# Half-height row tiles in the feed-forward products of a float32 transformer block on one Trainium2 core

## The chip, the cores and the metric

One of the eight cores of a Trainium2 chip runs the whole program. The metric is the device time of one launch in microseconds (us), as the median of the runs shown. Inputs and outputs are float32 in device memory. TensorE (PE in the profile) multiplies, VectorE (DVE), ScalarE (ACT) and GpSimd (POOL) do the element-wise work, and SyncE (SP) issues the transfers.

## The reference

A pre-layer-norm block over 2048 rows of 448 columns: multi-query attention with 16 heads of 28, then a SwiGLU feed-forward of width 1792.

```python
h  = x + A(_layernorm(x), wq, wk, wv, wo)        # attention, not touched by the change
h2 = h + B(_layernorm(h), w1, w3, w2)

def _B_ref(x, w1, w3, w2):                       # x 2048x448, w1 and w3 448x1792, w2 1792x448
    gate = jnp.einsum("bsd,df->bsf", x, w1)
    up   = jnp.einsum("bsd,df->bsf", x, w3)
    return jnp.einsum("bsf,fd->bsd", _silu(gate) * up, w2)
```

## The kernel before

Every float32 operand of a product is split into a high part, rounded to the matmul's float32r type, and a low part, the rest. A product of two such operands is the sum of three: high times high, low times high and high times low.

The rows of x are cut into 4 tiles of 512 (`t`), the feed-forward width into 14 chunks of 128 (`k`). The feed-forward runs over 4 x 14 = 56 blocks `(t, k)`, in order. In each block:

- `split_w` splits the columns of w1 and w3 for the chunk two blocks ahead (cast on VectorE, rest on GpSimd), and `split_w2` the rows of w2 for the next chunk. Split weights of w1 and w3 lie in a ring of seven `qs` buffers, those of w2 in the two places of `w2s`.
- `ffn1` makes the gate and the up products, each in a PSUM bank of its own (named `pa`), with `mm_D`: 448 contraction rows are three chunks of 128 and one of 64. The three chunks give 9 matmuls (three pairs of parts). For the last chunk the low part of x stands in partitions 0 to 63 and the high part in 64 to 127 of `xh[:, 3]`, and the weights stand there twice, so 2 matmuls do it. That is 11 matmuls of 512 columns for each bank, 22 in the block.
- Then ScalarE takes SiLU of the gate bank, VectorE multiplies it with the up bank, ScalarE rounds the result (`h[:, 0]`) and VectorE subtracts it to get the low part (`h[:, 1]`). These four steps write the tiles `pt`.
- `ffn2` takes the hidden part of the previous block (`prev`) times w2, into four banks `Y` (named `pb`) of 128 rows by 448 columns: 4 x 3 = 12 matmuls. `Y` collects over the 14 chunks of a row tile. After its last chunk `y_out` adds each bank to `X` on VectorE, and SyncE stores it.

Pieces of other work are hung on blocks in the table `after`: the output projection of the last attention rows (`wo_rows`, 11 full matmuls each), statistics and normalisation of the next row tile (`ln_stats`, `ln_norm`), and its transposes (`ln_tr`, 4 matmuls for each 128 columns, one column group in each of the blocks 5 to 8).

Seven PSUM banks are handed out by `bank`, which takes the free one whose last use is expected to end first. The eighth held the attention's output.

In the attention, the scores and row maxima (`Head.mm` and `Unit.mm`, lines 367 and 283) already use TensorE in four tiles of 32 rows, with up to four matmuls next to each other. All matmuls of the feed-forward use the full 128 rows.

Of the kernel before, what the change touches and what calls it, by code (L numbers as in the profile page):

```python
# [8 lines left out]
F32 = mybir.dt.float32  # L9
F32R = mybir.dt.float32r  # L10
AF = mybir.ActivationFunctionType
ALU = mybir.AluOpType
# [4 lines left out]
P = 128  # L17
S = 2048
D = 448
# [3 lines left out]
T = 512  # L23
NT = S // T
NQ = T // P
NG = H // 4
NC = S // P
NF = F // P
# [7 lines left out]
def block_kernel(  # L36
# [13 lines left out]
    ve, se, ge, pe, sy = nc.vector, nc.scalar, nc.gpsimd, nc.tensor, nc.sync  # L50
# [4 lines left out]
    def f(ap):  # L55
        return ap.bitcast(F32)
# [24 lines left out]
    W13, W2 = {}, dict(enumerate(W2_0))  # L81
    homes, n_qs = list(range(4)), [0]

    def qs_tile():
        k, n_qs[0] = homes[n_qs[0] % len(homes)], n_qs[0] + 1
        return keep.tile([P, 2, T], F32R, name="qs", tag=f"q{k}")
# [51 lines left out]

    clock, ready = Clock(), {}
    free, used = list(range(7)), {}  # L140
    order = [0.0] * 7

    def bank(name="pb"):
        k = min(free, key=lambda k: order[k])
        free.remove(k)
        ps = ps_w.tile([P, T], F32, name=name, tag=f"bank{k}")
        used[id(ps)] = ps, k
        ready.pop(id(ps), None)
        return ps

    def done(ps, at=None):
        k = used.pop(id(ps))[1]
        order[k] = ready.get(id(ps), clock.end) + 0.7 if at is None else at
        free.append(k)
# [29 lines left out]
    LN = {}  # L184
# [28 lines left out]
    XT = {}  # L213

    def xt_tiles():
        return [xt_pool.tile([P, m, T], F32R, name=name) for m, name in ((4, "xh"), (3, "xl"))]
# [11 lines left out]
    def ln_tr(t, c, spare=False):  # L228
        ps = last = TB[c] if TB else bank()
        if c == 0:  # L230
            XT[t] = xt_tiles()
        xh, xl = XT[t]
        r, c0 = (slice(0, P), c * P) if c < 3 else (slice(64, P), D - P)
        xns = LN[t][3]
        for n in range(NQ):
            if TB:
                break
            pe.transpose(ps[:, n * P : (n + 1) * P], xns[n][:, c0 : c0 + P], ident)  # L238
            clock.mm("full", 0, ps, 0.109, n == 0)
        se.activation(xh[r, c], ps[r], AF.Copy)  # L240
        eng = ve
        if spare:
            x32 = wk_pool.tile([P, T], F32, name="rb")
            se.activation(x32[r], ps[r], AF.Copy)
            eng, ps = ge, x32
        if c < 3:
            eng.tensor_tensor(xl[:, c], ps, f(xh[:, c]), op=ALU.subtract)
        else:
            eng.tensor_tensor(xh[:64, 3], ps[r], f(xh[r, 3]), op=ALU.subtract)
        if TB and c == 3:  # L250
            TB.clear()
        done(last)


    QS, MX, MR, PT, PO, WH, WS = {}, {}, {}, {}, {}, {}, {}
# [17 lines left out]
    class Unit:  # L273
# [22 lines left out]
        def plain(self):  # L296
            self.ps = self.mm()
            self.red()
# [102 lines left out]
    def o_norm(g):  # L401

        sm, sd = SM.pop(g), dr_pool.tile([4, T], F32, name="sd")
        ve.reciprocal(sm, sm)
        sy.dma_start(sd.rearrange("j (b e) -> (j b) e", b=32), sm)
        rb = RB[g] = wk_pool.tile([P, T], F32, name="rb")
        for j in range(4):
            sy.dma_start(rb[32 * j : 32 * j + 32], sd[j : j + 1].to_broadcast([32, T]))
# [37 lines left out]
    w2s_home = []  # L446

    def split_w2(k):
        if k == 0 and not w2s_home:
            w2s = qs_tile()  # L450
        else:
            if not w2s_home:
                w2s_home.append(keep.tile([P, 2, 2, T], F32R, name="w2s", tag="ks1"))
            w2s = w2s_home[0][:, k % 2]
        ve.tensor_copy(w2s[:, 0, :D], W2[k])
        ge.tensor_tensor(w2s[:, 1, :D], W2[k], f(w2s[:, 0, :D]), op=ALU.subtract)
        return w2s

    PAIRS = (0, 1)
# [10 lines left out]
    with tc.tile_pool(name="start", bufs=1) as sp:  # L470
# [106 lines left out]
        first = plain(0, 0, 0) + plain(0, 0, 1) + diffs(0, 0, 2) + plain(0, 1, 1) + sums(0, 0, 2) + plain(0, 1, 0) + diffs(0, 0, 3) + sums(0, 0, 3) + diffs(1, 0, 0) + sums(1, 0, 0) + plain(0, 2, 0) + plain(0, 2, 2) + plain(0, 2, 1) + plain(0, 3, 2) + plain(0, 3, 0) + diffs(0, 2, 3) + sums(0, 2, 3) + plain(0, 3, 1) + [(max_done, 0)] + diffs(1, 2, 0) + [(max_rows, 0), (max_out, 0)] + sums(1, 2, 0)  # L577
# [12 lines left out]
        po = ps_o.tile([P, T], F32, name="po")  # L590
# [189 lines left out]
    def pt_ring():  # L780
        k, n_ring[0] = n_ring[0] % 4, n_ring[0] + 1
        return pt_new(k)
# [20 lines left out]
    for t in range(NT - 1):  # L803
# [6 lines left out]
        for n in range(NQ):  # L810
# [8 lines left out]
            late = NC * NG * (t + 2) + 14 if t < 2 else LAST - 12  # L819
# [16 lines left out]
    for s in range(AHEAD, LAST):  # L836
        i, c = divmod(s, NC)
        n, kt = divmod(c, NQ)
# [7 lines left out]
    units = [0] + [64 - 4 * (AHEAD - NC)] + [64] * (NI - 2)  # L846
# [119 lines left out]

    HID, Y = {}, {}
    o_norm(NG - 1)

    def ffn1(t, k, W):  # L970
        ps = [bank("pa"), bank("pa")]
        for m in range(2):
            mm_D(ps[m], ps[m], [w[:, :, 1 - m] for w in W], XT[t], slice(0, P), slice(0, T))
        sg = f(pt_ring()[:, 0])
        se.activation(sg, ps[0], AF.Silu)  # L975
        done(ps[0])
        ve.tensor_tensor(sg, ps[1], sg, op=ALU.mult)  # L977
        done(ps[1])
        h = pt_ring()
        se.activation(h[:, 0], sg, AF.Copy)  # L980
        ve.tensor_tensor(h[:, 1], sg, f(h[:, 0]), op=ALU.subtract)  # L981
        HID[t, k] = h[:, 0], h[:, 1]

    def ffn2(t, k, n):
        if n == 0 and k == 0:
            Y[t] = [bank() for _ in range(NQ)]
        hid, w2s = HID[t, k], WS[t, k]
        for m, (a, b) in enumerate(((0, 0), (1, 0), (0, 1))):
            pe.matmul(Y[t][n][:, :D], hid[a][:, n * P : (n + 1) * P], w2s[:, b, :D],  # L989
                      start=(k == 0 and m == 0), stop=(k == NF - 1 and m == 2))  # L990

    def y_out(t, n):
        ve.tensor_tensor(X[t][:, n], Y[t][n][:, :D], X[t][:, n], op=ALU.add)  # L993
        done(Y[t][n])
        if t == NT - 1:
            sy.dma_start(ov[t][:, n], X[t][:, n])
        elif n == NQ - 1:
            sy.dma_start(ov[t], X[t])

    tl = NT - 1  # L1000
    after = {}

    def on(t, k, fn, *args):
        after.setdefault((t, k), []).append((fn, args))

    on(0, 0.5, o_mul, tl, NG - 1)
    on(0, 2, o_split, tl, NG - 1, lambda o, i: se.activation(o, i, AF.Copy), ve)
    for k in range(2):
        on(0, 2.5, load_w13, 2 * tl + k)
    for n in range(NQ):  # L1010
        on(0, 3 + n / 2, wo_rows, tl, n)
        on(0, 5 + n, ln_stats, tl, n)
    on(0, 4.5, put_late)
    for k in range(8, NF):
# [3 lines left out]
    for t in range(1, NT):  # L1018
        for n in range(NQ):
            on(t - 1, 1 + n, ln_norm, t, n)  # L1020
        for c in range(4):
            on(t - 1, 5 + c, lambda t, c: ln_tr(t, c), t, c)

    prev = None
    for t in range(NT):
        for k in range(NF):
            end = t == tl and k >= NF - 2
            t2, k2 = divmod(NF * t + k + 2, NF)
            if t2 < NT:
                WH[t2, k2] = split_w(k2)  # L1030
            ffn1(t, k, WH.pop((t, k)))
            for fn, args in after.get((t, k), []):
                fn(*args)
            if prev is not None and not end:
                for n in range(NQ):
                    ffn2(*prev, n)
                if prev[1] == NF - 1:
                    for n in range(NQ):
                        y_out(prev[0], n)
            t2, k2 = divmod(NF * t + k + 1, NF)  # L1040
            if t2 < NT and not end:
                WS[t2, k2] = split_w2(k2)
            for fn, args in after.get((t, k + 0.5), []):
                fn(*args)
            prev = (t, k)
    for n in range(NQ):
        ffn2(tl, NF - 3, n)
# [34 lines left out]
```

## Time and profile before

| | |
|---|---|
| median of 3 runs | 1179.75 us (1178.96 to 1179.86) |
| the profiled execution | 1180.76 us, of which the span of the profile is 1179.0 us |
| TensorE busy | 1168.7 us, 99% of the span |
| TensorE weight loads | 748.5 us, 63%, beside the matmuls |
| VectorE, ScalarE, GpSimd busy | 784.5, 745.1 and 325.3 us |
| attention | up to 742 us |
| feed-forward | from 742 us to the end |

Line numbers are those of the kernel before. In the profile a matmul's own time overlaps with the next one's, so what a matmul costs is read from how far apart starts lie, or from the chain of work that ended last, which gives each piece the time until the next one took over. PEld is the load of the stationary operand. A name such as `pb<-w2s,pt` says which tile is written and which are read.

### The profile page before, as it was taken

How to read it: one execution, taken by the hardware profiler on the slowest of the kernel's cores; microseconds unless marked ns; L12 is line 12 of the kernel's file. 1: busy time of each engine (PE TensorE's matmuls, PEld its weight loads, DVE VectorE, ACT ScalarE, POOL GpSimd, SP SyncE). 2: the span in 40 equal slices, each digit the busy share in tenths (PEclk: the TensorE clock that was granted, in tenths of full speed). 3: DMA queues.
4: the chain of work that ended last, by engine and by line, in shares of the span. 5: the costliest groups of instructions: out<-in, count | busy, mean ns of one | idle time of the engine just before them, and what ended most of it. 6: DMA issues, size and time to landing. Idle time of an engine off the chain costs nothing.

```text
span 1179.0 us, 22184 instructions
## 1 busy us (share of the span) xinstructions
PE 1168.7 (99%) x8618; PEld 748.5 (63%) x8618; DVE 784.5 (67%) x1479; ACT 745.1 (63%) x1435; POOL 325.3 (28%) x240
## 2 busy tenths in 40 slices
PE   8999999999999999999999999999999999999998
PEld 6664444445444445444455443788888888888887
DVE  7878999897899988989987961454343333333332
ACT  5649999996999997999997999312112211211111
POOL 5312001111110111110113013335555445455552
PEclk9999999999999999999999999999999999999999
DMA  4010100011000001000011000242000000000000
GB/s 165 10 37 1 42 10 11 19 22 39 19 19 5 16 24 38 19 19 13 9 39 35 6 18 19 70 113 69 1 32 1 1 4 28 1 1 32 1 1 31
DMA packets 35049, 30.58 MB, mean 26 GB/s; under 512 B 11904, under 2 KB 29568, under 8 KB 34944
## 3 DMA queue, kind: packets, MB, share of 16 engines
q1 hardware_dynamic: 34944, 29.17, 8.6%
q8 instruction: 67, 1.10, 0.4%
q14 instruction: 38, 0.31, 0.1%
HBM read 20.37 MB, written 3.80 MB: 20 GB/s over the span
## 4 chain that ended last, share of the span: by engine, by line
PE 93%; ACT 2%; DVE 2%; DMA 1%; issue 1%; SPq 0%; POOLq 0%; POOL 0%; ACTq 0%; DVEq 0%
PE pa L163 26%; PE po L383 21%; PE pb L367 20%; PE pb L989 11%; PE pa L283 10%; PE pb L163 4%; PE pb L238 1%; ACT OT L390 1%; DVE mx L293 1%; ACT ab L304 1%; ACT pt L374 0%; DMA sd<-sm 0%; DMA X<-in_A_x_dram 0%; DVE pt L981 0%; DVE X L993 0%
## 5 line engine op out<-in xcount | busy, mean ns | idle before, releaser
L293 DVE TENSOR_REDUCE mx<-pa 128x1 f32<-128x512 f32 x689 | 440.4, 685 | 21.9 <-PE pb L367 12.9
L367 PE MATMUL pb<-qs,KS 32*128 32x512 f32 x3072 | 385.3, 425 | 0.0
L374 ACT ACTIVATE pt<-pb 128x512 f32<-128x512 f32 x684 | 365.9, 620 | 12.5 <-PE pb L367 9.4
L367 PEld LDWEIGHTS pb<-qs,KS 32*128 32x128 f32 x3072 | 233.9, 182 | 133.4 <-ACT pt L374 68.1
L283 PE MATMUL pa<-KS,qs 32*128 32x512 f32 x886 | 312.1, 459 | 1.4
L163 PE MATMUL pa<-xh,qs 128*128 128x512 f32 x896 | 231.2, 390 | 0.0
L283 PEld LDWEIGHTS pa<-KS,qs 32*128 32x128 f32 x886 | 138.9, 182 | 82.8 <-DVE mx L293 46.4
L163 PEld LDWEIGHTS pa<-xh,qs 128*128 128x128 f32 x896 | 168.1, 188 | 33.8 <-issue 0.8
L383 PE MATMUL po<-pt,VA 128*32 128x512 f32 x1368 | 182.2, 604 | 0.4 <-ACT pt L374 0.4
L977 DVE TENSOR_TENSOR pt<-pa,pt 128x512 f32<-128x512 f32 x56 | 38.7, 691 | 206.9 <-PE pa L163 202.3
L975 ACT ACTIVATE pt<-pa 128x512 f32<-128x512 f32 x56 | 33.5, 599 | 193.0 <-PE pa L163 193.0
L989 PE MATMUL pb<-w2s,pt 128*128 128x448 f32 x660 | 144.4, 367 | 1.0 <-DVE pt L981 0.8
L414 POOL TENSOR_TENSOR OT<-OT,rb 128x512 f32<-128x512 f32 x15 | 19.2, 1282 | 456.3 <-DMA rb<-sd 251.6
L980 ACT ACTIVATE pt<-pt 128x512 fp32r<-128x512 f32 x56 | 35.4, 632 | 153.6 <-DVE pt L977 149.4
L989 PEld LDWEIGHTS pb<-w2s,pt 128*128 128x128 f32 x660 | 122.9, 188 | 13.4 <-DVE pt L981 1.2
L311 DVE CUSTOM_DVE_ANT_0 ab<-pa,ab 128x512 f32<-128x512 f32 x138 | 93.7, 687 | 39.8 <-PE pa L283 32.6
L374 ACT ACTIVATE xl<-pb 128x512 f32<-128x512 f32 x170 | 99.5, 609 | 7.6 <-PE pb L367 5.5
L374 ACT ACTIVATE xh<-pb 128x512 f32<-128x512 f32 x170 | 104.2, 631 | 0.0
L163 PE MATMUL pa<-xl,qs 128*128 128x512 f32 x336 | 94.5, 389 | 0.0
L383 PE MATMUL po<-xh,VA 128*32 128x512 f32 x340 | 89.4, 605 | 0.0
L383 PE MATMUL po<-xl,VA 128*32 128x512 f32 x340 | 89.4, 605 | 0.0
L304 ACT ACTIVATE ab<-pa 128x512 f32<-128x512 f32 x138 | 82.3, 608 | 6.6 <-PE pa L283 4.8
(109 smaller groups left out, 1088.8 us busy)
## 6 DMA issues: line engine op xcount, KB each, us to landing
rb<-sd SPq DMA_DIRECT2D x64, 64.0 KB
QR<-OT SPq DMA_DIRECT2D x60, 56.0 KB
QR<-in_B_w_dram SPq DMA_DIRECT2D x16, 192.0 KB
X<-in_A_x_dram SPq DMA_DIRECT2D x3, 896.0 KB
out_dram<-X SPq DMA_DIRECT2D x3, 896.0 KB
w<-in_B_w_dram SPq DMA_DIRECT2D x8, 192.0 KB
w_wo<-in_B_w_dram SPq DMA_DIRECT2D x6, 224.0 KB
qs<-mr SPq DMA_DIRECT2D x64, 2.0 KB
```

What stands on the lines that cost most here:

```text
L163: pe.matmul(ps, lhs[b][:, cb, lsl], rhs[a][:, ca, rsl], start=(k == 0), stop=(k == len(terms) - 1),)
L283: pe.matmul(ps, QS[i][r, 0, n * P : (n + 1) * P], KS[0][r, kt * T : (kt + 1) * T] if keys is None else keys[r], start=True, stop=True)
L293: ve.tensor_reduce(self.to(), ps, axis=AX.X, op=ALU.max)
L304: se.activation(self.ab, ps, AF.Relu)
L311: ve.tensor_tensor_reduce(self.ab, ps, self.ab, 1.0, -3.0e38, ALU.add, ALU.max, self.to())
L367: pe.matmul(self.ps, KS[k % 2][r, c * P : (c + 1) * P], QS[i][r, k // 2], start=(k == 0), stop=(k == 2))
L374: se.activation(f(PT[i, c, p][:, jj]), self.ps, AF.Exp, bias=0.0, scale=SCALE)
L383: pe.matmul(PO[i][32 * j : 32 * j + 32], VA[:, c], f(PT[i, c, j // 2][:, j % 2]), start=(c == 0), stop=(c == NC - 1))
L975: se.activation(sg, ps[0], AF.Silu)
L977: ve.tensor_tensor(sg, ps[1], sg, op=ALU.mult)
L980: se.activation(h[:, 0], sg, AF.Copy)
L989: pe.matmul(Y[t][n][:, :D], hid[a][:, n * P : (n + 1) * P], w2s[:, b, :D], start=(k == 0 and m == 0), stop=(k == NF - 1 and m == 2))
```

## The change

Fifty of the 56 blocks, from block 4 of the first row tile to block 11 of the last, are done in tiles of 64 contraction rows. TensorE is used as two halves: half 0 works on partitions 0 to 63, half 1 on 64 to 127, and `two` issues their matmuls in turn, one for each half, into different banks.

The order in such a block is: phase one of the first product (`ffn1_half`, gate in half 0 and up in half 1, 11 matmuls each), phase one of the second product of the previous block (`ffn2_half`, 6 each), phase two of the first (up in half 0 and gate in half 1, 10 each), the element-wise chain (`hidden`), phase two of the second (6 each). Counted in pairs, that is 21 pairs of 512 columns and 12 pairs of 448 columns.

Each bank is thus written by one half in one phase and by the other half in the other. Between the phases `settle` has ScalarE read one element of the bank into a scratch tile, and the next phase's first matmul into that bank waits for that read.

For the 64 last contraction rows half 0 also needs the high part of x, which stands in partitions 64 to 127: `put_xd` copies it down once for each row tile (ScalarE).

The transposes of the next row tile are done in halves too (`tr_half`, two column groups in each of blocks 5 and 7, half of them in each phase). `y_out` leaves two of the four banks of the first three row tiles to ScalarE (copy to `xn`) and GpSimd (addition), and in that block `y_out` stands between the multiplication and the rounding of the hidden part. The eighth bank is handed out as well. Each split part of w2 starts 16 floats further on in its buffer. Two pieces of `wo_rows` move from the steps 4 and 4.5 of the first row tile to 3 and 3.5.

```diff
+    order[7] = clock.end + 4
...
+    def two(pairs):
+        for units in zip(*pairs):
+            for h, (ps, lhs, rhs, first, last) in enumerate(units):
+                pe.matmul(ps[:, : rhs.shape[-1]], lhs, rhs, start=bool(first), stop=bool(last), skip_group_check=True)
...
+    def settle(ps):
+        se.activation(pexp[:1, 8:9], ps[:1, :1], AF.Copy)
...
+    def products(t, W, m, h):
+        r = HALF[h]
+        u = [(W[b][r, c, 1 - m], XT[t][a][r, c]) for a, b in PAIRS3 for c in range(3)]
+        return u + [(W[0][r, 3, 1 - m], XT[t][0][r, 3])]
+
+    def ffn1_half(t, k, W, ps, late):
+        us = [products(t, W, late, 0), products(t, W, 1 - late, 1)]
+        if not late:
+            extra = W[1][HALF[0], 3, 1], XD[0][HALF[0]]
+            us[0].insert(0 if k == NF - 1 else len(us[0]), extra)
+            us[1].append((W[1][HALF[1], 3, 0], XT[t][0][HALF[1], 3]))
...
+    def ffn2_half(t, k, late):
...
+        for h in range(2):
+            for n0 in (2, 0) if late else (0, 2):
+                n, r = n0 + (h ^ late), HALF[h]
+                for m, (a, b) in enumerate(PAIRS3):
+                    us[h].append((Y[t][n], hid[a][r, n * P : (n + 1) * P], w2s[r, b],
...
+        two(us)
+        settle(Y[t][0 if late else 3])
...
     def y_out(t, n):
-        ve.tensor_tensor(X[t][:, n], Y[t][n][:, :D], X[t][:, n], op=ALU.add)
+        y, eng = Y[t][n][:, :D], ve
+        if t < NT - 1 and n > 1:
+            y, eng = ln_pool.tile([P, 512], F32, name="xn", bufs=4)[:, :D], ge
+            se.activation(y, Y[t][n][:, :D], AF.Copy)
+        eng.tensor_tensor(X[t][:, n], y, X[t][:, n], op=ALU.add)
...
+                ps = [bank("pa"), bank("pa")]
+                ffn1_half(t, k, W, ps, 0)
+                call(between, t, k)
+                ffn2_half(*prev, 0)
+                ffn1_half(t, k, W, ps, 1)
+
+                def rest():
+                    ffn2_half(*prev, 1)
+                    call(behind, t, k)
+                    if prev[1] == NF - 1:
+                        for n in range(NQ):
+                            y_out(prev[0], n)
+
+                hidden(t, k, ps, rest if prev[1] == NF - 1 else None)
+                call(after, t, k)
+                if prev[1] != NF - 1:
+                    rest()
```

The order of TensorE in one block before: `pa` are the two banks of the first product, `xh` and `xl` the high and low part of x, `qs` the split w1 and w3, `pt` the hidden part.

```order
L163 MATMUL pa<-xh,qs 128x512 x3
L163 MATMUL pa<-xl,qs 128x512 x3
L163 MATMUL pa<-xh,qs 128x512 x8
L163 MATMUL pa<-xl,qs 128x512 x3
L163 MATMUL pa<-xh,qs 128x512 x5
L989 MATMUL pb<-w2s,pt 128x448 x12
```

One block now, from the fifth matmul of `ffn2_half`'s first phase to the block's end, with what a row waits for on other engines. Each row holds matmuls of both halves in turn, and all banks have the same names as before:

```order
L992 MATMUL pb<-w2s,pt 128x448 [waits Pool_49]
L992 MATMUL pb<-w2s,pt 128x448 x7
L992 MATMUL pa<-xh,qs 128x512 [waits Activation_49]
L992 MATMUL pa<-xh,qs 128x512 x5
L992 MATMUL pa<-xl,qs 128x512 x6
L992 MATMUL pa<-xh,qs 128x512 x8
L992 MATMUL pb<-w2s,pt 128x448 [waits Activation_49]
L992 MATMUL pb<-w2s,pt 128x448 x11
```

The 22 matmuls of the first product became two runs of 22 and 20 half-height ones, of which the second stands here, between two runs of 12 of the second product; the first matmul of a run now waits for ScalarE, whose `settle` reads one of its banks after the run before.

VectorE around the last addition of the first row tile, before: `X_77` is that row tile, `pt<-pa,pt` the multiplication and `pt<-pt` the subtraction of the hidden part.

```order
L977 TENSOR_TENSOR pt<-pa,pt 128x512
L981 TENSOR_TENSOR pt<-pt 128x512
L993 TENSOR_TENSOR X_77<-pb,X_77 128x448 x4
L455 CAST w2s<-w2r_100 128x448
L442 CAST qs<-QR_89 128x1024
```

And now, at the same place:

```order
L1002 TENSOR_TENSOR pt<-pa,pt 128x512
L1079 TENSOR_TENSOR X_77<-pb,X_77 128x448 x2
L1008 TENSOR_TENSOR pt<-pt 128x512
L462 CAST w2s<-w2r_100 128x448
L449 CAST qs<-QR_89 128x1024
```

Two of the four additions left VectorE, and the other two moved ahead of the subtraction that ends the hidden part.

More of the change, by code (lines that the diff above doesn't have):

```diff
@@ L140, in block_kernel @@
     free, used = list(range(7)), {}
-    order = [0.0] * 7
+    order = [0.0] * 8
     def bank(name="pb"):
@@ L145, in bank @@
         free.remove(k)
-        ps = ps_w.tile([P, T], F32, name=name, tag=f"bank{k}")
+        if k < 7:
+            ps = ps_w.tile([P, T], F32, name=name, tag=f"bank{k}")
+        else:
+            ps = ps_o.tile([P, T], F32, name="po")
         used[id(ps)] = ps, k
@@ L231, in ln_tr @@
             XT[t] = xt_tiles()
-        xh, xl = XT[t]
-        r, c0 = (slice(0, P), c * P) if c < 3 else (slice(64, P), D - P)
+        c0 = c * P if c < 3 else D - P
         xns = LN[t][3]
@@ L239, in ln_tr, with to_x @@
             clock.mm("full", 0, ps, 0.109, n == 0)
+        to_x(t, c, ps, last, spare)
+    def to_x(t, c, ps, last, spare=False):
+        xh, xl = XT[t]
+        r = slice(0, P) if c < 3 else slice(64, P)
         se.activation(xh[r, c], ps[r], AF.Copy)
@@ L449, in split_w2 @@
         if k == 0 and not w2s_home:
-            w2s = qs_tile()
+            w2s = qs_tile()[:, :, 16 : 16 + D]
         else:
@@ L453, in split_w2 @@
                 w2s_home.append(keep.tile([P, 2, 2, T], F32R, name="w2s", tag="ks1"))
-            w2s = w2s_home[0][:, k % 2]
-        ve.tensor_copy(w2s[:, 0, :D], W2[k])
-        ge.tensor_tensor(w2s[:, 1, :D], W2[k], f(w2s[:, 0, :D]), op=ALU.subtract)
+            w2s = w2s_home[0][:, k % 2, :, 16 : 16 + D]
+        ve.tensor_copy(w2s[:, 0], W2[k])
+        ge.tensor_tensor(w2s[:, 1], W2[k], f(w2s[:, 0]), op=ALU.subtract)
         return w2s
@@ L968, in block_kernel, with put_xd, hidden @@
     o_norm(NG - 1)
[L970 to L973, printed above, removed]
+    free.append(7)
+    order[7] = clock.end + 4
+    HALF = (slice(0, 64), slice(64, 128))
+    PAIRS3 = ((0, 0), (1, 0), (0, 1))
+    FULL = 4
+    XD = {}
+    def put_xd(t):
+        if not XD:
+            XD[0] = wk_pool.tile([P, T], F32R, name="rb")
+        se.activation(XD[0][:64], f(XT[t][0][64:, 3]), AF.Copy)
+    def two(pairs):
+        for units in zip(*pairs):
+            for h, (ps, lhs, rhs, first, last) in enumerate(units):
+                pe.matmul(ps[:, : rhs.shape[-1]], lhs, rhs, start=bool(first), stop=bool(last), skip_group_check=True)
+                clock.mm("half", h, ps, 0.016 + rhs.shape[-1] / 2400, first)
+    def settle(ps):
+        se.activation(pexp[:1, 8:9], ps[:1, :1], AF.Copy)
+    def hidden(t, k, ps, then=None):
         sg = f(pt_ring()[:, 0])
@@ L978, in ffn1 @@
         done(ps[1])
+        if then is not None:
+            then()
         h = pt_ring()
@@ L982, in ffn1 @@
         HID[t, k] = h[:, 0], h[:, 1]
+    def ffn1(t, k, W):
+        ps = [bank("pa"), bank("pa")]
+        for m in range(2):
+            mm_D(ps[m], ps[m], [w[:, :, 1 - m] for w in W], XT[t], slice(0, P), slice(0, T))
+        hidden(t, k, ps)
+    def products(t, W, m, h):
[8 more added lines that the diff above has]
+            us[1].append((W[1][HALF[1], 3, 0], XT[t][0][HALF[1], 3]))
+        to = (ps[0], ps[1]) if not late else (ps[1], ps[0])
+        two([[(to[h], *u, not late and x == 0, late and x == len(us[h]) - 1) for x, u in enumerate(us[h])]
+             for h in range(2)])
+        if not late:
+            settle(ps[1])
     def ffn2(t, k, n):
@@ L987, in ffn2, with tr_half @@
         hid, w2s = HID[t, k], WS[t, k]
-        for m, (a, b) in enumerate(((0, 0), (1, 0), (0, 1))):
-            pe.matmul(Y[t][n][:, :D], hid[a][:, n * P : (n + 1) * P], w2s[:, b, :D],
-                      start=(k == 0 and m == 0), stop=(k == NF - 1 and m == 2))
-    def y_out(t, n):
-        ve.tensor_tensor(X[t][:, n], Y[t][n][:, :D], X[t][:, n], op=ALU.add)
+        for m, (a, b) in enumerate(PAIRS3):
+            pe.matmul(Y[t][n][:, :D], hid[a][:, n * P : (n + 1) * P], w2s[:, b],
+                      start=(k == 0 and m == 0), stop=(k == NF - 1 and m == 2), skip_group_check=True)
+    def ffn2_half(t, k, late):
+        if k == 0 and not late:
+            Y[t] = [bank() for _ in range(NQ)]
+        hid, w2s = HID[t, k], WS[t, k]
+        us = [[], []]
+        for h in range(2):
+            for n0 in (2, 0) if late else (0, 2):
+                n, r = n0 + (h ^ late), HALF[h]
+                for m, (a, b) in enumerate(PAIRS3):
+                    us[h].append((Y[t][n], hid[a][r, n * P : (n + 1) * P], w2s[r, b],
+                                  not late and k == 0 and m == 0, late and k == NF - 1 and m == 2))
+        two(us)
+        settle(Y[t][0 if late else 3])
+    TR = {}
+    def tr_half(t, cs, late):
+        if not late:
+            for c in cs:
+                TR[c] = bank()
+        for n in range(NQ):
+            for h in range(2):
+                c = cs[h ^ late]
+                c0, r = (c * P if c < 3 else D - P), HALF[h]
+                pe.transpose(TR[c][:, n * P + 64 * h : n * P + 64 * h + 64], LN[t][3][n][r, c0 : c0 + P], ident[r, r])
+                clock.mm("half", h, TR[c], 0.109, n == 0)
+        if late:
+            for c in cs:
+                if c == 0:
+                    XT[t] = xt_tiles()
+                to_x(t, c, TR[c], TR[c])
+    def y_out(t, n):
+        y, eng = Y[t][n][:, :D], ve
[3 more added lines that the diff above has]
+        eng.tensor_tensor(X[t][:, n], y, X[t][:, n], op=ALU.add)
         done(Y[t][n])
@@ L1000, in block_kernel, with on, call @@
     tl = NT - 1
-    after = {}
-    def on(t, k, fn, *args):
-        after.setdefault((t, k), []).append((fn, args))
+    after, between, behind = {}, {}, {}
+    def on(t, k, fn, *args, to=after):
+        to.setdefault((t, k), []).append((fn, args))
+    def call(to, *at):
+        for fn, args in to.get(at, []):
+            fn(*args)
     on(0, 0.5, o_mul, tl, NG - 1)
+    on(0, 1, put_xd, 0)
     on(0, 2, o_split, tl, NG - 1, lambda o, i: se.activation(o, i, AF.Copy), ve)
@@ L1010, in block_kernel @@
     for n in range(NQ):
-        on(0, 3 + n / 2, wo_rows, tl, n)
+        on(0, FULL - 1 + n // 2 / 2, wo_rows, tl, n)
         on(0, 5 + n, ln_stats, tl, n)
@@ L1020, in block_kernel @@
             on(t - 1, 1 + n, ln_norm, t, n)
-        for c in range(4):
-            on(t - 1, 5 + c, lambda t, c: ln_tr(t, c), t, c)
+        for p in range(2):
+            for late in range(2):
+                on(t - 1, 5 + 2 * p, tr_half, t, (2 * p, 2 * p + 1), late, to=behind if late else between)
+        on(t - 1, NF - 1, put_xd, t, to=between)
     prev = None
@@ L1030, in block_kernel @@
                 WH[t2, k2] = split_w(k2)
[L1031 to L1037, printed above, removed]
-                    for n in range(NQ):
-                        y_out(prev[0], n)
+            W = WH.pop((t, k))
+            if t == 0 and k < FULL or end:
+                ffn1(t, k, W)
+                call(after, t, k)
+                if prev is not None and not end:
+                    for n in range(NQ):
+                        ffn2(*prev, n)
+            else:
+                ps = [bank("pa"), bank("pa")]
+                ffn1_half(t, k, W, ps, 0)
[6 more added lines that the diff above has]
+                    if prev[1] == NF - 1:
+                        for n in range(NQ):
+                            y_out(prev[0], n)
+                hidden(t, k, ps, rest if prev[1] == NF - 1 else None)
+                call(after, t, k)
+                if prev[1] != NF - 1:
+                    rest()
             t2, k2 = divmod(NF * t + k + 1, NF)
@@ L1042, in block_kernel @@
                 WS[t2, k2] = split_w2(k2)
-            for fn, args in after.get((t, k + 0.5), []):
-                fn(*args)
+            call(after, t, k + 0.5)
             prev = (t, k)
```

## The prediction

> **What bounds the kernel now.** I read the page's first part, then the stages by windows, then the chain that ended last. The first two show which engine is full in the stage that the change touches.
>
> ```profile
> PE 1168.7 (99%) x8618; PEld 748.5 (63%) x8618; DVE 784.5 (67%) x1479; ACT 745.1 (63%) x1435; POOL 325.3 (28%) x240
> ```
>
> ```profile
> 800.00:900.00 100.00, 100.00 (x467) 85.86 (x466) 39.19 (x73) 18.48 (x31) 50.80 (x28) 1.00 0.07 22
> 900.00:1000.00 100.00, 100.00 (x464) 85.73 (x463) 37.81 (x67) 17.79 (x30) 49.38 (x26) 1.00 0.03 10
> 1000.00:1100.00 100.00, 100.00 (x466) 85.62 (x465) 35.97 (x61) 18.07 (x30) 51.12 (x28) 1.00 0.02 10
> ```
>
> In each 100 us of the feed-forward TensorE is busy for 100 (columns: PE, PEld, DVE, ACT, POOL, then granted clock, transfers). ScalarE works 18 of them, VectorE 38, GpSimd 50. The chain shows the same in pieces, one block after the other:
>
> ```profile
> 863.53 5.00 PE pa L163 x22
> 868.53 2.43 PE pb L989 x12
> 870.97 5.00 PE pa L163 x22
> 875.97 2.43 PE pb L989 x12
> ...
> 906.22 0.44 PE pb L238 x4
> 906.65 2.47 PE pb L989 x12
> 909.13 5.04 PE pa L163 x22
> ```
>
> A block is 5.00 + 2.43 = 7.43 us, all of it matmuls that follow each other: 5.00/22 = 0.2273 us for 512 columns and 2.43/12 = 0.2025 us for 448. Weight loads hide. So the change counts by two things: what TensorE issues, and what it newly waits for.
>
> **What a pair of halves costs.** A block now has 21 pairs of 512 columns and 12 of 448. The gain is one slot of 22, less whatever a pair costs over a full matmul; the trace of before has no tile of 64 rows. Its nearest rows on one side are the full matmuls above, on the other the attention's tiles of 32 rows, four next to each other. The timeline of TensorE in three growing windows from 718.15, and a longer run:
>
> ```profile
> 718.15 0.50 PE L367 MATMUL pb<-qs,KS 32*128 32x512 f32 x4
> ...
> 718.15 0.74 PE L367 MATMUL pb<-qs,KS 32*128 32x512 f32 x8
> ...
> 718.15 0.98 PE L367 MATMUL pb<-qs,KS 32*128 32x512 f32 x12
> ...
> 723.84 1.42 PE L367 MATMUL pb<-qs,KS 32*128 32x512 f32 x16
> ```
>
> Four tiles make a turn. One turn takes 0.50 us with its start and end, two 0.74, three 0.98: 0.24 a turn. In the run of 16 one tile has five matmuls: (1.42 - 0.50)/4 = 0.23. So tiles do run next to each other, and a turn of four costs 0.23 to 0.24 us, where a full matmul costs 0.2273. Two tiles should lie between. I take 0.230 for 512 columns, the lower of the two row-tile readings, since it is taken over the longer run, and for 448 columns the same 0.0027 over the full one: 0.205.
>
> - Block: 21 x 0.230 + 12 x 0.205 = 4.83 + 2.46 = 7.29 us, 0.14 less than 7.43. Over 50 blocks: **-7.0 us**.
> - At the full matmul's price: 21 x 0.2273 + 12 x 0.2025 = 7.20, -0.23 a block, -11.3 us.
> - At 0.24 and 0.215: 5.04 + 2.58 = 7.62, +0.19 a block, +9.5 us.
>
> Each nanosecond on a pair is 33 x 50 = 1650 pairs, 1.65 us. That price decides the sign.
>
> The Trainium skill (TensorE: Matmul & The Clock Gate, Part 3, "Measured speedup vs the span model") gives 3.07 times for four row tiles of 32 rows, so by it a turn of four would be 4/3.07 = 1.30 full matmuls, an estimate of 0.296 us against the trace's 0.23 to 0.24, which does not agree. If a pair cost those 1.30 matmuls, the estimate by that page would be some 110 us more than my sum.
>
> **What the new order makes TensorE wait for.** The hidden part, from one block's timeline and two group rows:
>
> ```profile
> 881.00 0.60 ACT L975 ACTIVATE pt<-pa 128x512 f32<-128x512 f32 x1 [3.57 <-PE pa L163]
> ...
> 882.11 1.30 PE L163 MATMUL pa<-xh,qs 128*128 128x512 f32 x5
> ...
> 883.51 0.69 DVE L977 TENSOR_TENSOR pt<-pa,pt 128x512 f32<-128x512 f32 x1 [4.02 <-PE pa L163]
> 884.23 0.63 ACT L980 ACTIVATE pt<-pt 128x512 fp32r<-128x512 f32 x1 [2.63 <-DVE pt L977]
> 884.90 0.69 DVE L981 TENSOR_TENSOR pt<-pt 128x512 fp32r<-128x512 f32 x1 [0.70 <-ACT pt L980]
> ```
>
> ```profile
> L163 PE MATMUL pa<-xh,qs 128*128 128x512 f32 x695 | 179.7, 390 | 0.0
> L163 PEld LDWEIGHTS pa<-xh,qs 128*128 128x128 f32 x696 | 130.7, 188 | 25.6
> ```
>
> The last matmul (0.39 us long by its group, with a weight load of 0.19) ends at 882.11 + 1.30 = 883.41, VectorE starts 0.10 later and the low part is done at 885.59. Now both banks end together, so SiLU (0.60, and 0.04 to the next) comes into the chain: 0.10 + 0.60 + 0.04 + 2.08 = 2.82 us after the end. TensorE needs the low part for its second pair of `ffn2_half`; until then it has 6 x 0.205 + 11 x 0.230 + 0.205 and the last pair's own 0.23, less its 0.39: 3.81, and the weights are loaded 0.19 ahead: 3.6. The slack is 0.8 us (before, a whole `ffn1` lay between). Nothing is lost in a plain block.
>
> The `settle` reads: nearest is ScalarE's smallest copy.
>
> ```profile
> L468 ACT ACTIVATE pexp<-pexp 128x8 f32<-128x8 f32 x1 | 0.2, 208 | 0.0
> L240 ACT ACTIVATE xh<-pb 128x512 fp32r<-128x512 f32 (+1 forms) x32 | 19.0, 600 | 9.2 <-PE pb L238 7.3 <-PE pb L225 1.7
> ```
>
> ```profile
> L993 DVE TENSOR_TENSOR X<-pb,X x16: 614/616/625, 863.6 to 1175.4; 128x448 f32<-128x448 f32 x16
> L989 PEldq EVENT_SEMAPHORE  x4: 51/51/51, 864.3 to 1171.7; - x4
> ```
>
> Three in each block, 0.21 each, fit ScalarE's 82% of idle time; queued behind them there stand SiLU and the rounding, which come later anyway. The tightest, after phase one of `ffn1_half`, needs 0.10 + 0.21 + 0.04 + 0.19 = 0.54 us, and six pairs of the second product give 1.23 + 0.23 - 0.39 = 1.07. Hidden; without that cover it would be 0.5 us a block, 27 us.
>
> Three places do wait, by the same rows:
>
> - The three `y_out` blocks. The last pair of the old `Y` ends 1.23 us after the first product; then 0.10, a `settle` 0.21, two bank copies on ScalarE (0.60 each, L240 above), the rounding 0.63, the subtraction 0.69 and 0.1 between them: 4.2 us against 3.6. 3 x 0.6 = 1.8. VectorE's two additions (0.616 each) run beside the copies, GpSimd's beside later work.
> - The six halves of transposes. They hold two banks, so the next block takes the banks that the multiplication has just left, free at 0.10 + 0.60 + 0.04 + 0.69 = 1.43; TensorE comes with its loads at 1.23 + 0.23 - 0.39 + 4 x 0.11 - 0.19 = 1.3. 6 x 0.15 = 0.9. The transposes themselves: 4 full ones take 0.44 (0.11 each); 16 halves are 8 pairs, at 0.11 as much as the 8 full ones they replace; bounds are half of that and nothing, 0 to -2.6 us, and I take 0.
> - Separate waits on TensorE's queue: the built program has 40 more, at 0.051 each. They stand ahead of a load that can start 0.04 us early, so 0 to 2.0 us; I take 0.
>
> Moving two `wo_rows` changes nothing in their number. `put_xd` (0.6 us of ScalarE, four times) lies in its idle time. The place of w2 in its buffer: between nothing and the 448-column matmul's excess over 512 columns' share, 0.2025 - 0.2273 x 448/512 = 0.0036, times 600 = -2.2 us; a loss has no row. I take 0.
>
> Sum: -7.0 + 1.8 + 0.9 = **-4.3 us**. The profiled execution took 1180.76, so its like would take 1176.5; the median of the runs, 1179.75, lies 1.0 lower, so I say **1175.4**.
>
> **The rivals.** A difference of 0.2%, 2.4 us, is about what a measurement here can tell from none.
>
> - *Forecast, 0.50*: pairs at 0.227 to 0.231. 1168.4 (-11.3, no waits) to 1177.
> - *A wash, 0.18*: pairs at 0.231 to 0.234. With 2.7 us of waits the break-even is 0.230 + 4.3/1650 = 0.2326. For it: the turn of four reads 0.23 to 0.24. 1177 to 1182.
> - *Dear pairs, slower, 0.22*: one mechanism, the change of weights inside a tile. Each pair must wait for the slower of two halves; at the 0.24 of the short turns the sum is +9.5 + 2.7 = +12.2, 1192. It decides above 0.2341 (2.4 us over break-even). Against it: two tiles have fewer to wait for than four.
> - *A new wait in every block, slower, 0.07*: the hidden part's slack is used up. For it, this step of the chain, where VectorE's subtraction lasted longer beside GpSimd:
>
> ```profile
> 759.03 1.80 DVE pt L981
> ```
>
>   With 1.80 for 0.69 the slack of 0.8 becomes a stall of 0.3 a block: +15 - 4.3, 1191. Against it: from 800 on GpSimd starts after the subtraction, as the new order keeps it.
> - *Loads in the open, 0.03*: the next weights of a half do not load under its running matmul. Then every pair pays what the first turn of a run pays over a single matmul, 0.50 - 0.39 = 0.11: 0.11 x 1650 = +181, 1357. Against it: the second and third turn above do not pay it. This is the direction of the Trainium skill's 3.07 in the section named above.
>
> That the halves are not used together has no chance to speak of: four tiles are, in the rows above.
>
> **How the numbers follow.** Faster is the forecast with 0.03 of the wash, 0.53; the rest of the wash is the same, 0.15; slower are the last three, 0.32. The forecast's own range is 1168.4 to 1177; to leave out no more than 2 in 10 the range goes up into the dear pairs, to 0.239: 1175.4 + 9 x 1.65 = 1190.
>
> **What would show it.** Chain or timeline after: a run of 22 halves at 11 x 0.230 = 2.53 us and 12 at 1.23, a plain block at 7.29. Above 7.38 a block the gain is gone. In the waits, TensorE behind ScalarE or VectorE should total under 4 us; more than 0.1 us in each block means that the slack was misjudged. A block that spreads evenly over 7.4 us without waits means dear pairs.

## The result, and the profile after

| | before | changed |
|---|---|---|
| median | 1179.48 us of 4 runs (1178.96 to 1179.86) | 1169.21 us of 4 runs (1168.05 to 1169.86) |
| ratio | | 0.9911, 95% interval 0.9899 to 0.9923 |
| the profiled execution, its span | 1180.76, 1179.0 us | 1168.05, 1166.2 us |

The change made the kernel 10.3 us faster; -4.3 was forecast, to 1175.4. TensorE is the bound as before. The page's first part after, and the same three windows of the feed-forward (columns: PE, PEld, DVE, ACT, POOL):

```profile
PE 1155.6 (99%) x10266; PEld 772.7 (66%) x10266; DVE 781.1 (67%) x1473; ACT 768.7 (66%) x1595; POOL 334.0 (29%) x246
```

```profile
800.00:900.00 100.00, 100.00 (x934) 96.05 (x933) 40.83 (x74) 25.57 (x76) 55.25 (x32) 1.00 0.03 11
900.00:1000.00 100.00, 100.00 (x934) 95.82 (x932) 36.11 (x62) 25.14 (x75) 55.46 (x30) 1.00 0.03 10
1000.00:1100.00 100.00, 100.00 (x924) 96.19 (x923) 35.82 (x61) 24.31 (x74) 56.23 (x30) 1.00 0.03 11
```

TensorE still has no gap in these windows. It runs twice as many matmuls in 100 us, and loads of weights are under way 96 of 100 us instead of 86. What became shorter is the block. TensorE's timeline over one block of the changed kernel and the start of the next (each row is a run of like matmuls; L992 is `two`):

```profile
816.04 0.88 PE L992 MATMUL pa<-xh,qs 64*128 64x512 f32 x6
816.73 0.88 PE L992 MATMUL pa<-xl,qs 64*128 64x512 f32 x6
817.42 1.10 PE L992 MATMUL pa<-xh,qs 64*128 64x512 f32 x8
818.33 0.39 PE L992 MATMUL pa<-rb,qs 64*128 64x512 f32 x1
818.36 0.39 PE L992 MATMUL pa<-xh,qs 64*128 64x512 f32 x1
818.57 1.39 PE L992 MATMUL pb<-w2s,pt 64*128 64x448 f32 x12
819.76 0.88 PE L992 MATMUL pa<-xh,qs 64*128 64x512 f32 x6
820.44 0.90 PE L992 MATMUL pa<-xl,qs 64*128 64x512 f32 x6
821.12 1.12 PE L992 MATMUL pa<-xh,qs 64*128 64x512 f32 x8
822.03 1.42 PE L992 MATMUL pb<-w2s,pt 64*128 64x448 f32 x12
823.24 0.39 PE L992 MATMUL po<-xh,qs 64*128 64x512 f32 x1
```

From start to start: 11 pairs of 512 columns take 818.57 - 816.04 = 2.53 us, 6 pairs of 448 columns 1.20, 10 pairs 2.27, 6 pairs 1.21, and the block 823.24 - 816.04 = **7.20 us**, against 7.43 before and 7.29 forecast. That is 4.80/21 = 0.229 us for a pair of 512 columns and 2.41/12 = 0.201 for one of 448. With 50 such blocks 0.23 each is 11.5 us. From the start of its first matmul to the start of its last the feed-forward took 432.8 us in the trace before and 421.0 after, 11.8 less; the two spans differ by 12.8, 1.0 of it in the attention, which the change doesn't touch. In a second trace of the changed kernel, from the runs under "The place of w2" below, the feed-forward takes 420.9 us again but starts at 743.9 instead of 741.2 us. So single executions can scatter by 2.7 us in the attention alone, more than what separates 11.8 from the 10.3 of the medians.

The waits of the changed kernel, for the load side of TensorE from 742 us to the end (us in total, times, longest; short waits are not listed), show that the new order costs next to nothing:

```profile
PEld pb L1039 <- DVE pt L1008: 0.9, 1, 0.9
PEld po L1039 <- POOL w2s L463: 0.6, 1, 0.6
PEld pb L992 <- DVE pt L1008: 0.4, 2, 0.2
PEld po L992 <- issue: 0.3, 1, 0.3
PEld pa L166 <- issue: 0.3, 1, 0.3
PEld po L992 <- DVE pt L1008: 0.2, 1, 0.2
```

None is on ScalarE's `settle` reads. The third and the last row are three waits of 0.2 us for the subtraction behind `y_out`; the first two belong to the last blocks, which are done as before.

### The profile page after: what moved, and what is told of

It is laid out like the page before. It is cut to its first block, busy times and chain, and to the rows that moved or that the text cites. A ratio compares the mean times of both kernels' runs of the same rounds, so it can differ in the third digit from the quotient of the medians.

```text
span 1166.2 us, 25723 instructions
## 1 busy us (share of the span) xinstructions
PE 1155.6 (99%) x10266; PEld 772.7 (66%) x10266; DVE 781.1 (67%) x1473; ACT 768.7 (66%) x1595; POOL 334.0 (29%) x246
## 4 chain that ended last, share of the span: by engine, by line
PE 92%; DVE 2%; ACT 2%; DMA 1%; issue 1%; SPq 1%; POOLq 0%; ACTq 0%; DVEq 0%
PE po L390 21%; PE pb L374 20%; PE pa L992 18%; PE pa L290 10%; PE pb L992 9%; PE pa L166 4%; PE pb L166 4%; PE po L992 4%; DVE mx L300 1%; ACT OT L397 1%; ACT ab L311 1%; PE pb L240 1%; PE pb L1039 1%; DMA OT<-in_A_wq_dram 0%; ACT pt L381 0%
## 5 line engine op out<-in xcount | busy, mean ns | idle before, releaser
L992 PE MATMUL pa<-xh,qs 64*128 64x512 f32 x1262 | 214.0, 388 | 0.0
L992 PEld LDWEIGHTS pa<-xh,qs 64*128 64x128 f32 x1262 | 158.2, 184 | 6.2
L1002 DVE TENSOR_TENSOR pt<-pa,pt 128x512 f32<-128x512 f32 x50 | 34.6, 691 | 180.5 <-ACT pt L1000 174.2
L992 PE MATMUL pb<-w2s,pt 64*128 64x448 f32 x1050 | 142.4, 361 | 0.0
L992 PEld LDWEIGHTS pb<-w2s,pt 64*128 64x128 f32 x1050 | 121.4, 184 | 3.0 <-DVE pt L1008 0.4
L992 PE MATMUL pa<-xl,qs 64*128 64x512 f32 x522 | 90.8, 388 | 0.0
L1000 ACT ACTIVATE pt<-pa 128x512 f32<-128x512 f32 x48 | 28.7, 599 | 93.0 <-PE pa L992 88.9
L450 POOL TENSOR_TENSOR qs<-QR,qs 128x1024 fp32r<-128x1024 f32 x32 | 76.5, 2393 | 15.2 <-DVE qs L449 15.2
```

The source lines that it names most:

```text
L450: ge.tensor_tensor(wl, W13[k], f(wh), op=ALU.subtract)
L992: pe.matmul(ps[:, : rhs.shape[-1]], lhs, rhs, start=bool(first), stop=bool(last), skip_group_check=True)
```

## The experiments

The theory after the result: a pair of halves costs one full matmul of the same width, so the gain is the slot that is saved in each block, 21 in place of 22, and the waits are covered. The rivals: the new place of w2 makes a part of the gain; halves gain by something else than the slot; the price comes with the number of tiles next to each other, as the prediction assumed.

**One more pair.** One pair is added to the second run of the first product.

```diff
             us[1].append((W[1][HALF[1], 3, 0], XT[t][0][HALF[1], 3]))
+        else:
+            us[0].append((W[1][HALF[0], 0, 0], XT[t][1][HALF[0], 0]))
+            us[1].append((W[1][HALF[1], 0, 1], XT[t][1][HALF[1], 0]))
```

> The changed kernel with one more pair of halves in each of the 50 half-height blocks: low part of x times low part of w, first chunk, added to both banks, so 22 pairs as there were 22 full matmuls. The theory that the gain is the saved slot: a plain block goes from 7.20 by 0.23 to 7.43, the 7.43 of before, and the time by 11.4 us to 1180.6, the time of before. The rival, that halves gain by something else too (shorter waits, weight loads): the block stays well under 7.43 and a part of the gain is left.

Measured: 1179.32 us, ratio to before 0.9998 (0.9988 to 1.0008). Its timeline:

```profile
816.95 0.88 PE L992 MATMUL pa<-xh,qs 64*128 64x512 f32 x6
...
822.95 0.44 PE L992 MATMUL pa<-xl,qs 64*128 64x512 f32 x2
823.17 1.42 PE L992 MATMUL pb<-w2s,pt 64*128 64x448 f32 x12
824.38 0.39 PE L992 MATMUL po<-xh,qs 64*128 64x512 f32 x1
```

The row at 822.95 holds the added pair; the block is 824.38 - 816.95 = 7.43 us, and the whole gain is gone. So the gain is that slot, and nothing else in the halves pays. (This kernel has w2 at its new place; the kernel before with w2 there, below, has 7.42 a block and 1177.90 us, so 22 pairs are no cheaper than 22 full matmuls.)

**One half alone.** Half 1 is left out but for the first and the last matmul of each run and the first into a bank; the output lacks those products.

```diff
-        for units in zip(*pairs):
+        for x, units in enumerate(zip(*pairs)):
             for h, (ps, lhs, rhs, first, last) in enumerate(units):
+                if h and 0 < x < len(pairs[0]) - 1 and not first:
+                    continue
```

> The changed kernel with nearly all matmuls of half 1 left out in the half-height blocks (only the first and the last of each run are kept, and the first into a bank), so that half 0 streams almost alone; the output lacks those products. It gives the price of a tile of 64 rows by itself. Theory C (a half costs what a full matmul costs, and a second half beside it nothing): the runs of 11 and 10 stay at 2.53 and 2.27, the six at 1.20, a block at 7.20, 1169. Theory D (the price comes with the number of tiles that run next to each other, since a pair waits for the slower half): the runs fall, by 1 ns or more a slot, towards 0.2257 or below and the block under 7.17. Neither: a half alone is dearer.

Measured: 1167.15 us in one run. TensorE's timeline, a block from its start to the next (L994 is the same line):

```profile
830.43 0.85 PE L994 MATMUL pa<-xh,qs 64*128 64x512 f32 x3
831.13 0.85 PE L994 MATMUL pa<-xl,qs 64*128 64x512 f32 x3
...
837.63 0.62 PE L994 MATMUL pa<-xh,qs 64*128 64x512 f32 x2
```

From 830.43 to 837.63 is 7.20 us a block again, to the digit. A half by itself costs what the pair costs, and the second half beside it adds nothing: theory C. The prediction's thought that a pair must wait for the slower of two halves has no effect here that can be seen.

**The place of w2.** Back at the start of its buffer, in the changed kernel, and moved as the change moves it, in the kernel before.

```diff
-            w2s = qs_tile()[:, :, 16 : 16 + D]
+            w2s = qs_tile()[:, :, :D]
...
-            w2s = w2s_home[0][:, k % 2, :, 16 : 16 + D]
+            w2s = w2s_home[0][:, k % 2, :, :D]
```

> The changed kernel with the split w2 back at the start of its buffer, as before. Theory A (the place does nothing; the price of a pair of halves is that of the tiles alone): a run of six pairs of 448 columns stays at 1.20 to 1.21 us, a plain block at 7.20, and the time at about 1169. Theory B (the place of w2 is part of the gain: with it a 448-column pair is 0.2007 us, under the 0.2025 of a full matmul): the run of six goes to 1.215 or more, a plain block to 7.22 or more, the time up by 1 us or more. Beyond 7.43 a block, the place would carry the whole gain.

> The kernel before, in full height, with nothing changed but the place of the split w2, 16 floats further on. Theory A: 12 full matmuls of 448 columns stay at 2.43 us and the time at 1179.5. Theory B: they go to 12 x 0.2007 = 2.41 or below, and the time falls by 56 x 0.02 = 1 us or more; it would then be a gain that needs no halves.

Measured: with halves 1168.24 us, ratio to before 0.9903 (0.9890 to 0.9917), no slower than the changed kernel. In full height 1177.90, ratio 0.9987 (0.9978 to 0.9996): 1.6 us faster. First the changed kernel with w2 at the start (timeline), then the kernel before with w2 moved (chain):

```profile
815.72 0.86 PE L992 MATMUL pa<-xh,qs 64*128 64x512 f32 x6
...
818.24 1.38 PE L992 MATMUL pb<-w2s,pt 64*128 64x448 f32 x12
819.45 0.87 PE L992 MATMUL pa<-xh,qs 64*128 64x512 f32 x6
...
822.95 0.39 PE L992 MATMUL pa<-xh,qs 64*128 64x512 f32 x1
822.96 0.39 PE L992 MATMUL po<-xh,qs 64*128 64x512 f32 x1
```

```profile
950.66 2.41 PE pb L989 x12
953.07 5.01 PE pa L163 x22
```

In full height 12 matmuls of 448 columns take 2.41 us instead of 2.43 and 22 of 512 columns 5.01 instead of 5.00. So a plain block is 7.42 instead of 7.43, and the blocks with transposes, by the starts of their first matmuls, 7.88 instead of 7.95. With halves at the old place six pairs take 819.45 - 818.24 = 1.21 and the block 822.95 - 815.72 = 7.23. So the matmuls of 448 columns do get cheaper, by about 1% in full height and by less in halves, and theory B is right for them. As the first pair of medians left the time open, both kernels ran once more on one chip:

> The changed kernel once more, beside the next one on the same chip: 1168 to 1170.

> The changed kernel with the split w2 at the start of its buffer, once more, beside the changed kernel. In its first run a plain block was 7.225 against 7.200 in the trace, 1.2 us over 50 blocks, and the median was 1.0 us lower, not higher. If the place counts with halves too, it is slower than the changed kernel here by about 1 us; if not, the two medians lie within 0.6 us.

Measured: 1169.73 (ratio 0.9914, 0.9902 to 0.9926) and 1169.99 us (0.9917, 0.9903 to 0.9931). In the time of the half-height kernel the place makes no difference that can be measured. The traces show a small one: from the first matmul of the first half-height block to the first matmul behind the last one, the 50 blocks take 366.3 and 366.4 us with w2 moved (778.26 to 1144.57 and 780.78 to 1147.15) and 366.9 and 367.0 with it at the start (777.86 to 1144.78 and 779.46 to 1146.45). That is 0.6 us, less than the 0.03 of a plain block times 50, since the blocks behind `y_out`, which wait, are 7.37 with w2 at the start and 7.43 with it moved, and the last of the 50 is 7.4 and 7.6. The halves' own gain has to be read with w2 at one place in both kernels. At the start it is 1179.5 to 1168.2 and 1179.6 to 1170.0, 11.3 and 9.6 us; moved it is 1177.9 to 1169.2 or 1169.7, 8.7 and 8.2 us. So is the price of a pair: at the start the prices of full height give 7.20 for 33 matmuls where the block has 7.23, and moved they give 5.01 x 21/22 + 2.41 = 7.19 where it has 7.20. A pair of halves costs a full matmul to within 0.4%.

**The phases in a row.** The cover between a `settle` read and the matmul that waits for it is taken away.

```diff
                 call(between, t, k)
-                ffn2_half(*prev, 0)
                 ffn1_half(t, k, W, ps, 1)
+                ffn2_half(*prev, 0)
```

> The changed kernel with both phases of the first product behind each other, then both of the second, so that nothing lies between a settle read and the matmul that waits for it. By the prediction's step each of the two phase changes in a block then shows 0.10 + 0.16 + 0.04 + 0.19 and the end of the last matmul, 0.5 to 0.65 us: 50 to 65 us in all, 1220 to 1235. The rival, that the wait costs nothing because the loads and matmuls of the other half go on: less than 0.1 us a block, under 1175.

Measured: 1224.66 us in one run. Its timeline, the wait in brackets, and the waits of its load side:

```profile
881.96 0.39 PE L992 MATMUL pa<-xh,qs 64*128 64x512 f32 x1
882.66 0.96 PE L992 MATMUL pa<-xh,qs 64*128 64x512 f32 x6 [0.32 <-ACT pexp L996]
```

```profile
PEld pb L992 <- ACT pexp L996: 33.1, 48, 0.7
PEld pa L992 <- ACT pexp L996: 28.3, 41, 0.7
```

The first matmul of phase two starts 0.70 us after the last of phase one, where 0.23 is a slot. Both phase changes together make the block 8.39 to 8.45, 1.2 us more than 7.20. The waits listed are for `settle` reads (`pexp`). So the read costs 0.6 us where nothing covers it, and with such reads the interleaving of the two products is what makes the halves pay at all.

**A longer hidden chain.** The subtraction is made three times.

```diff
-        ve.tensor_tensor(h[:, 1], sg, f(h[:, 0]), op=ALU.subtract)
+        for _ in range(3):
+            ve.tensor_tensor(h[:, 1], sg, f(h[:, 0]), op=ALU.subtract)
```

> The changed kernel with the last subtraction of the hidden part made three times instead of once, in the 50 half-height blocks and the six others, the same values again. Each adds 0.61 to 0.69 us to the chain. By the prediction's step the slack of a plain block is 0.8 us (0.87 in the trace after), so 1.22 to 1.38 more leaves a wait of 0.35 to 0.55 us in each block: 17 to 28 us, 1186 to 1197. The rival, that the slack is far larger because the second pair is not what waits: no change, 1169. If the slack had been none: 61 to 69 us.

Measured: 1206.20 us in one run, more than expected. VectorE's timeline in it, the same in the changed kernel, and the waits of its load side:

```profile
934.09 2.14 DVE L1009 TENSOR_TENSOR pt<-pt 128x512 fp32r<-128x512 f32 x3 [0.70 <-ACT pexp L996]
```

```profile
838.76 0.69 DVE L1008 TENSOR_TENSOR pt<-pt 128x512 fp32r<-128x512 f32 x1 [0.70 <-ACT pexp L996]
```

```profile
PEld pb L992 <- DVE pt L1009: 25.7, 34, 2.5
PEld po L992 <- DVE pt L1009: 9.8, 11, 2.5
```

Three take 2.14, so two more add 1.45, not the 1.22 to 1.38 that was expected; why each added one takes a little more was not tried. A plain block became 7.80 to 7.84, 0.6 more than 7.20: the slack is 1.45 - 0.6 = 0.85 us, close to the prediction's 0.8. That makes some 30 of the 37 us. Most of the rest is in the three blocks behind `y_out` (9.5 to 11.2 us instead of 7.43), which wait 2.5 us each for the subtraction.

**The additions as before.**

```diff
-        if t < NT - 1 and n > 1:
+        if False:
...
-                hidden(t, k, ps, rest if prev[1] == NF - 1 else None)
+                hidden(t, k, ps)
...
-                if prev[1] != NF - 1:
-                    rest()
+                rest()
```

> The changed kernel with y_out as it was before: all four additions on VectorE, behind the whole hidden chain of the block. The theory, that y_out comes at the price of the blocks that follow it (0.23 us of waiting in each of three blocks now): four additions of 0.62 free the four banks later and TensorE waits for banks or for the next split; 0.5 to 1 us more in each of three blocks, 1.5 to 3 us in all, 1171 to 1172. The rival: the hidden part comes earlier than now, the three waits of 0.23 go away, 1168.5.

Measured: 1170.94 us, ratio to before 0.9923 (0.9906 to 0.9939), where the changed kernel has 0.9911; the intervals overlap. In the traces the block behind `y_out` is 8.25 us here and 7.43 in the changed kernel, three times 0.8, and from first to last matmul the feed-forward is 2.5 us longer (423.6). What TensorE waits for there is now the last additions:

```profile
PEld pb L992 <- DVE X L1079: 2.9, 3, 1.0
```

So the new form of `y_out`, its split over three engines and its earlier place taken together, is worth about 2.5 us by the traces; the two were not tried apart.

**Only the first product in halves.**

```diff
-                ffn2_half(*prev, 0)
+                for n in range(2):
+                    ffn2(*prev, n)
...
-                    ffn2_half(*prev, 1)
+                    for n in range(2, NQ):
+                        ffn2(*prev, n)
```

> The changed kernel with only the first product in halves: the second in full height, two banks after each phase, and the transposes in full height; four changes of tile shape in each block. If a change of shape is free: 2.53 + 2.27 + 2.43 = 7.23 us a block, 1171. If a change of shape drains TensorE (in the attention, 719.06 minus the last start of the row tiles 0.31 us before: about 0.1 us more than a turn): 0.1 to 0.2 each, 20 to 40 us in all, 1190 to 1210. The first would mean that the second product need not be in halves.

Measured: 1210.31 us in one run. Its timeline (L1039 is the full-height second product), and the largest waits of its load side:

```profile
860.89 0.97 PE L992 MATMUL pa<-xh,qs 64*128 64x512 f32 x6
...
863.63 1.48 PE L1039 MATMUL pb<-w2s,pt 128*128 128x448 f32 x6
865.05 0.97 PE L992 MATMUL pa<-xh,qs 64*128 64x512 f32 x6
```

```profile
PEld pb L1039 <- issue: 34.0, 95, 0.4
PEld pa L992 <- issue: 19.9, 70, 0.3
```

11 pairs now take 863.63 - 860.89 = 2.74 us instead of 2.53, six full matmuls 1.42 instead of 1.20. Each change of tile shape costs 0.2 us, four in a block 0.8 (8.06 us a block). It isn't a wait for another engine: with a third group, `po` (7.0 us, 24 times), the load side stands idle at 189 of the 200 changes, and "issue" says that it waited for nothing that the profile shows. Twelve pairs of the second product cost what its twelve full matmuls cost, so it gains nothing by halves for itself; it has to follow the first one's shape.

## Why the prediction was right, and where its sizes were off

The direction and the mechanism came out as forecast: one slot less in each block, with the waits covered. The size did not. The gain is 2.4 times the forecast, and faster had been given a chance of only 0.53. The three errors below all point the same way.

- *What bounds the kernel*: right. TensorE has next to no gap before or after, and the time follows its slots.
- *What a pair of halves costs*: the mis-sized term. Taken were 0.230 and 0.205 us, measured 0.229 and 0.201, 7.20 a block instead of 7.29, 4.5 us over 50 blocks. The step was "two tiles should lie between": the row of four tiles of 32 is no bound for two of 64. One half alone and both together give the same 7.20, so the price is that of a single matmul, and the full-height rows of before (7.20 by the prediction's own lower bound) were the right ones. The row of four tiles was also read too coarsely: in (1.42 - 0.50)/4 both figures are rounded to 0.01 us, which leaves 0.0025 us a turn open, 4 us over 1650 pairs. Of the 0.09 a block, 0.06 is the price (7.29 to 7.23, w2 at the start in the changed kernel) and 0.03 the place of w2 (7.23 to 7.20). For the place nothing was taken and up to -2.2 us allowed; the kernel before gains 1.6 by it, the 50 half-height blocks 0.6.
- *What the new order waits for*: the plain block right (slack 0.8 forecast, 0.85 shown; `settle` hidden, 0.5 to 0.6 each when not). The `y_out` blocks were forecast at 0.6 each and are 7.43 - 7.20 = 0.23. The timelines of ScalarE and VectorE show why:

```profile
859.75 0.95 ACT L1078 ACTIVATE xn<-pb 128x448 f32<-128x448 f32 x2
860.60 0.62 ACT L1007 ACTIVATE pt<-pt 128x512 fp32r<-128x512 f32 x1
861.25 0.81 DVE L1008 TENSOR_TENSOR pt<-pt 128x512 fp32r<-128x512 f32 x1 [0.22 <-ACT pt L1007]
```

  Two copies were put at 0.60 each; together they take 0.95, and the rounding starts 0.85 after the first of them: 0.35 us less in the chain. The subtraction took 0.81 instead of 0.69, and the `settle` read before the copies held them up by less than its 0.21 (0.07, from 859.68 to 859.75), which about cancel. That is 0.7 in place of 1.8 in all.
- *The transposes*: forecast at +0.9 for waits and 0 for themselves. By the starts of the blocks' first matmuls, blocks 5 to 9 of the second row tile took 39.22 us before (893.10 to 932.32), 2.05 more than plain ones, and 37.69 after (888.30 to 925.99), 1.69 more, so three row tiles gained 1.1. The wait is there. At the end of a block eight halves take 0.38 to 0.44 us until the next block starts, in its middle 0.22, and the next block's first load starts when VectorE's multiplication has left the bank, at 895.51 + 0.69 = 896.20:

```profile
895.51 0.69 DVE L1002 TENSOR_TENSOR pt<-pa,pt 128x512 f32<-128x512 f32 x1 [4.10 <-ACT pt L1000]
896.25 0.53 PEld L992 LDWEIGHTS pa<-xh,qs 64*128 64x128 f32 x6
```

  That is about 0.2 a time, near the 0.15 taken. But four pairs without it take the 0.22 of the block's middle, half of 4 x 0.11, which is the bound of -2.6 that the prediction had and didn't take.
- *The sum*: 4.5 + 1.1 + 2.0 = 7.6 us better than -4.3 makes -11.9, about the -11.8 of the traces. The measured 1169.21 lies inside the forecast's own range (from 1168.4) by 0.8 us, near the end that took the full matmul's price and no waits; the profiled execution, 1168.05, lies just outside. That this range held was close.
- *The rivals*: dear pairs and a wash by them are out by the extra pair and the single half. A new wait in every block did not come; the longer chain shows that 0.85 us of slack stood against it. Loads in the open are out: weight loads are under way 96% of the time, and the pairs keep the price of a full matmul. The Trainium skill (TensorE: Matmul & The Clock Gate, Part 3, "Measured speedup vs the span model") gives 3.07 times for four row tiles of 32 rows, which falls short of four. Two tiles of 64 rows fall short of nothing in this trace: twice the matmuls (934 for 467) in the same 100 us.

## What to carry to other kernels

A contraction that does not fill the last tile of the array (448 of 512 rows here) can be cut into half-height tiles run side by side: the pair costs one full matmul, and the saved slots are the gain. In this kernel it pays only because the two writers of a bank are kept apart by other matmuls, since ordering them through a ScalarE read costs 0.6 us in the open (whether they need to be ordered was not tried), and because everything in that stage keeps one tile shape, since each change costs 0.2. And where a term that the trace does not show is multiplied by 1650, read its nearest rows to the nanosecond before choosing between them: here 0.2273 and 0.230 were 4 to 5 us apart, more than the forecast change itself, and the runs came out near the first.

## What the runs showed of the hardware

- A block of 33 pairs of 64-row matmuls next to each other takes 7.20 us, and 7.20 with nearly all of one half left out.
- A change between full height and half height costs about 0.2 us (2.74 for 2.53, 1.42 for 1.20).
- Full-height matmuls whose moving operand of 448 columns starts 64 bytes further on in its buffer take about 1% less (12 of them 2.41 us for 2.43); why was not tried. With it the two halves can run apart from each other (the pair that starts at 823.24 and 823.30), without it almost in step (822.95 and 822.96).
- Four tiles of 32 rows in the attention start a new turn every 0.23 us (724.18, 724.41 and 724.64 in the run at 723.84). By unrounded starts twelve such turns of the trace before average 0.232, where a full matmul takes 0.227; why they take more stays open.
